# Four stream slots in place of five, one more granule at home, and edits to the first step and the tail

## The chip, the cores and the metric

The kernel runs on one core of a Trainium2 chip. Its time is device time in microseconds (us); three runs of the kernel before gave 1846.27, 1849.24 and 1857.47, and the median, 1849.24, is the figure to compare with. The profile is of one execution. TensorE (PE, with its weight loads as PEld), VectorE (DVE), ScalarE (ACT), GpSimd (POOL) and SyncE (SP) each work through their own instructions in program order, and DMA queues are fed by SP, ACT and POOL. The TensorE clock is granted by a throttle, and the profile shows the granted share as PEclk.

## The reference

`x` is 2048 rows of 1024 numbers. It is normalised (a layer norm without weights), goes through a recurrent attention (A) and through a routed MLP (B), and both are added to it.

```python
def _A_ref(x, mem0, Wq, Wk, Wv, Wo, seg_len):       # 64 segments of 32 rows, 32 heads of 128
    mem = mem0                                       # 8 rows of memory
    for s in range(n_seg):
        xs = x[:, s * seg_len:(s + 1) * seg_len, :].copy()
        h = jnp.concatenate([mem, xs], axis=1)       # 40 rows
        q, k, v = (einsum('btd,dhe->bhte', h, W) for W in (Wq, Wk, Wv))
        scores = jnp.einsum('bhqe,bhke->bhqk', q, k) * scale
        scores = jnp.where(mask[None, None], scores, -1000000000.0)
        o = jnp.einsum('bhqk,bhke->bhqe', _softmax(scores, axis=-1), v)
        o = jnp.einsum('bhte,hed->btd', o, Wo)
        mem = o[:, :M, :].copy()
        outs.append(o[:, M:, :])
    return jnp.concatenate(outs, axis=1)

def _B_ref(x, w_r, w_gate, w_up, w_down):            # the 2 rows with the largest router value
    r = x @ w_r
    idx = jnp.argsort(-r, axis=-1)[:, :C]
    x_sel = jnp.take_along_axis(x, idx_e, axis=1)
    y = (_silu(x_sel @ w_gate) * (x_sel @ w_up)) @ w_down
    ...                                              # times sigmoid(r), added to those rows

x = A_x
xn = _layernorm(x, axis=-1)
return x + _A_ref(xn, A_mem0, A_Wq, A_Wk, A_Wv, A_Wo, A_seg_len) + _B_ref(xn, B_w_r, B_w_gate, B_w_up, B_w_down)
```

Each segment needs the memory that the segment before it left, so the 64 segments run one after the other, and each reads all of Wq, Wk, Wv and Wo.

## The kernel before

**Steps and granules.** One pass of the loop in line 621 is a step: one segment. The weights are cut into 64 granules of 128 x 2048 numbers, 512 KB each. Granules 0 to 47 are Wq, Wk and Wv in six phases of eight (`PHASES`, line 26: Q first half, K first half, Q second half, K second half, V first half, V second half); granules 48 to 63 are Wo. In a phase the state `ST` (32 rows: 24 of x, 8 of memory) is the weight of the matmuls and the granule streams through it, four matmuls side by side (line 745). Line 754 takes a Q or K phase's sum out, line 632 turns it, lines 637 to 642 copy it to `QT` and `KT`. The Wo granules are used in line 798.

**Homes, slots and kept granules.** The on-chip memory can't hold all the weights. 44 granules (`N_RES`) have a home and are loaded once. Three (`KEPT_HERE`: 0, 7, 27) are kept turned in PSUM and brought back each step (line 411). The other 17 (`streamed`, line 77) go through a ring of five slots (`wstream`, `N_SLOT`). `fetch` (line 380) takes the next granule of the list `flow` and issues its load on SP (line 386 in the first step, 388 later, from scratch copies `wsc` that GpSimd makes in the first step). After step 0 a fetch is issued as soon as a streamed granule has been used (`after`, line 575), into that granule's slot, so it is the granule five places on in the list. SP runs in order: a fetch that waits for its slot holds back all that SP has behind it.

**Inside a step.** `hooks` places the attention's parts between granules: scores of the first heads after granule 22 (line 644), their softmax on VectorE and ScalarE (667 to 686), scores of the second heads after granule 38, the weighted sums (`attend`, line 688) after granules 43 and 46 and within the Wo granules. GpSimd loads the next rows of x, the left products (`QKL`) and `VL`.

**Left rows.** Only 24 of a segment's 32 rows go through the loop together with the 8 rows of memory. The last eight of each segment, 512 rows in all, are "left" rows: their products with Wq, Wk and Wv are made in the first step for all segments at once (`left_qk`, line 493, and `left_v`, line 521; in four sets of 128 rows), stored, and loaded per step. Their attention output is stored per step (`store_sums`), loaded back at the end into `OTA`, and multiplied by Wo in `left_rows_out` (line 868): two calls, each of two sets of 128 rows, 64 matmuls a set, the weights read from `OTR` with a stride of 32 numbers.

**First step.** Phase by phase, the eight granules are used for the step itself and then, still in place, for the left products; a slot is released only when both are done. `left_done(p)` (line 548) then fetches one granule for each slot of the phase that has come free, and reloads areas that served as scratch. The row statistics of all x tiles are made on VectorE (line 238); `spread` (line 245) hands them to the segments' rows; `router_tile` (line 261) makes the router value of 128 rows at a time, 16 times, and stands in phase 1, after three heads of left products. `hm` and `hx` are homes that serve as scratch first.

**Tail.** In the last step the homes that are done with take the expert weights (`fetch_moe`, line 429, on SP). `left_sums` (line 852) makes the statistics of the left rows again on VectorE from x loaded on ScalarE's queue (line 850); then come the first call of `left_rows_out`, gate and up products (line 903), the second call, the rest of gate and up, and down (line 930).

Of the kernel before, what the change touches and what calls it, by code (L numbers as in the profile page):

```python
# [8 lines left out]
BF16 = mybir.dt.bfloat16  # L9
# [7 lines left out]

N_RES = 44
N_SLOT = 5
FIRST_KEPT = 0  # L20
NEXT_KEPT = 7
HALF_KEPT = 27
KEPT_HERE = (FIRST_KEPT, NEXT_KEPT, HALF_KEPT)
NEG = -30000.0

# [4 lines left out]
def kernel(  # L30
# [45 lines left out]

    streamed = [1, 4, 11, 15, 21, 23, 29, 34, 37, 41, 45, 47, 50, 54, 56, 58, 63]
    first_streamed = sorted(streamed + list(KEPT_HERE))
# [181 lines left out]

    def router_tile(t):
        XR = home(hx, [P, D], BF16, "XR")
        nc.vector.tensor_scalar(out=XR[:, :], in0=xt(t), scalar1=RI16[:, t, 0:1], scalar2=RI16[:, t, 1:2],
                                op0=ALU.subtract, op1=ALU.mult)
        nc.vector.tensor_tensor_reduce(out=XR[:, :], in0=XR[:, :], in1=WRB, scale=1.0, scalar=0.0,
                                       op0=ALU.mult, op1=ALU.add, accum_out=RF[:, t:t + 1])

# [153 lines left out]
    to_copy = list(streamed)  # L421
    flow += [(s, g) for s in range(NSEG) for g in (streamed if s else first_streamed)]

# [54 lines left out]
    for g in range(KC, 32):  # L478
        if g in first_streamed:
            if len(queued) < N_SLOT:  # L480
                fetch()
        else:
            load_resident(g)
        if g >= 8 and g < 15:
            load_x(g - 7)
    for g in v_homes[8:-1]:
        load_resident(g)
# [5 lines left out]
    def left_qk(mat, half, Gs, between, h0=0, h1=16):  # L493
        if mat == 0 and h0 == 0:
            gathered[half] = area(f"big{half}", [P, NSEG, 256], "GA")
        GA = gathered[half].rearrange("p s (m i q r) -> p s m i q r", m=2, i=4, q=4)
        for h in range(h0, h1):
            PSG = psA.tile([P, 512], F32, tag="acc", name="PSG")
            for kc in range(KC):
                nc.tensor.matmul(PSG[:, :], lhsT=part(Gs[kc], h // 4)[:, P * (h % 4):P * (h % 4 + 1)], rhs=XLT[:, :, kc, :],  # L500
                                 start=(kc == 0), stop=(kc == KC - 1))
            nc.scalar.copy(out=GA[:, :, mat, h % 4, h // 4, :], in_=PSG.rearrange("p (s r) -> p s r", r=XL))  # L502
            if h % 2 == 1 or mat + half == 0:
                next(between, None)
        if h1 < 16:
            return
        for _ in between:
            pass
        if mat == 1:
            G3 = gathered[half]  # L510
            if half == 0:
                qkl[0] = one.tile([P, 2, 2, 4, 4, XL], BF16, tag="bA", name="QKL")
            nc.vector.tensor_copy(out=qkl[0][:, half].rearrange("p m i q r -> p (m i q r)"), in_=G3[:, 0, :])
            if half == 0:
                for k in range(NSEG // 8):
                    store_left(half, k)
# [104 lines left out]
    for s in range(NSEG):  # L621
# [7 lines left out]
        def transposes(mat, half, XB):  # L629
# [8 lines left out]
            else:  # L638
                KT[half] = one.tile([P, 16, NK], BF16, tag="kt", name="KT")
                nc.scalar.copy(out=KT[half].rearrange("p (i q) k -> p i q k", i=4)[:, :, :, 32:NK],  # L640
                               in_=qkl[0][:, half, 1, :, :, :])
                nc.vector.tensor_copy(out=KT[half][:, :, 0:32], in_=pv)  # L642

# [94 lines left out]
        for p, (mat, half) in enumerate(PHASES):  # L738
# [13 lines left out]
            if mat < 2:  # L752
# [4 lines left out]
                if s == 0:  # L757
# [94 lines left out]
    def left_sums():  # L852
# [7 lines left out]
        for t in range(4):  # L860
# [3 lines left out]
            nc.vector.tensor_scalar(out=left_x(t), in0=left_x(t), scalar1=r, scalar2=m, op0=ALU.mult, op1=ALU.add)  # L864

    OTR = OTA.rearrange("p s (r h) -> p (s r) h", h=H)

    def left_rows_out(k):
        WD = [[psK.tile([P, 512], F32, name=f"WD{2 * b + c}", tag=f"kept{2 * b + c}") for c in range(2)] for b in range(2)]
        for b in range(2):  # L870
            for i, (g, Gv) in enumerate(WOS.items()):
                for hs in range(2):
                    for c in range(2):
                        nc.tensor.matmul(WD[b][c][:, :], lhsT=OTR[:, P * (2 * k + b):P * (2 * k + b + 1), 2 * (g - 48) + hs],  # L874
                                         rhs=Gv[:, D * hs + 512 * c:D * hs + 512 * (c + 1)],
# [6 lines left out]

    T0 = room(resident[2], "T0")
    left_sums()
# [87 lines left out]
```

## Time and profile before

| what | value |
|---|---|
| time, median of 3 runs | 1849.24 us (1846.27 to 1857.47) |
| the profiled execution's own time | 1847.92 us |
| its span | 1846.3 us, mean granted clock 0.982 |
| TensorE busy | 1555.7 us (84%) |
| VectorE busy | 880.4 us (48%) |
| ScalarE busy | 774.9 us (42%) |
| GpSimd busy | 320.9 us (17%) |
| DMA moved | 678.50 MB, mean 367 GB/s |

The page's second part cuts the span into 40 slices of 46 us and gives the busy share of each in tenths, so a row of nines is a resource in use all the time. In a row of instructions, the first number is the start, the second the length (of all that are merged, where a count stands at the end), then engine, line, operation, the tiles written and read, shapes and count; in brackets stands the engine's idle time before and what ended it. A row of a waits view has the waiting instruction, what it waited for, the total, the number of times and the longest. A row of a windows view has the stretch, then for PE, PEld, DVE, ACT and POOL the busy time and count, then the granted clock, the DMA share and GB/s.

### The profile page before, as it was taken

The page shows a single profiled execution, that of the slowest core. Times are in us where ns is not written, and L with a number is a line of the kernel's source. Part 1 is how long each engine was busy: PE and PEld are TensorE (multiplying, and loading weights), DVE is VectorE, ACT ScalarE, POOL GpSimd, SP SyncE. Part 2 cuts the span into 40 slices and gives each one's busy share as a digit, 9 for nine tenths or more (in the row PEclk, how much of TensorE's full clock was granted, in tenths as well). Part 3 has the DMA queues.
Part 4 walks back from the last instruction along what each step waited for, and adds up shares of the span by engine and source line. Part 5 has one row for each costly group of instructions (what it writes and reads, how often), then busy time and mean ns, then how long its engine had stood idle before and what let it go on. Part 6 is the DMA issues. An engine that isn't in the chain of part 4 may idle for free. (4 is left out here: it accounts for less than half of the span.)

```text
span 1846.3 us, 70379 instructions
## 1 busy us (share of the span) xinstructions
PE 1555.7 (84%) x30358; PEld 828.2 (45%) x30370; DVE 880.4 (48%) x2711; ACT 774.9 (42%) x2019; POOL 320.9 (17%) x592
## 2 busy tenths in 40 slices
PE   6889978888888888888888888888888888888888
PEld 3334434444444444444444444444444444444465
DVE  6631235555554454555555555444455555555420
ACT  2333134444444444444444444444444444444400
POOL 1020111111111111111111111111111111111200
PEclk9999989999999999999999999999999999999988
DMA  9684899999999999999999999999999999999996
GB/s 361 218 301 135 261 367 391 393 394 394 368 387 376 368 389 383 392 386 372 396 393 396 396 394 394 385 386 389 386 391 394 397 382 393 395 395 395 392 364 251
DMA packets 223288, 678.50 MB, mean 367 GB/s; under 512 B 46848, under 2 KB 54320, under 8 KB 222976
## 3 DMA queue, kind: packets, MB, share of 16 engines
q1 hardware_dynamic: 196768, 623.79, 88.3%
q0 software_dynamic: 24192, 46.54, 7.5%
q8 instruction: 237, 3.88, 0.8%
q10 hardware_dynamic: 2016, 3.67, 0.6%
q14 instruction: 75, 0.61, 0.1%
HBM read 652.90 MB, written 29.89 MB: 370 GB/s over the span
## 5 line engine op out<-in xcount | busy, mean ns | idle before, releaser
L745 PE MATMUL PSm<-wres,ST 128*32 128x512 bf16 x6400 | 500.7, 382 | 0.0
L745 PEld LDWEIGHTS <-ST 128*32 128x32 bf16 x12288 | 313.3, 96 | 349.5 <-issue 107.4
L745 PE MATMUL PSm<-g,ST 128*32 128x512 bf16 x3084 | 307.3, 384 | 46.6 <-DMA g<-wsc 38.2
L411 ACT COPY BK<-KEPT 128x512 bf16<-128x512 bf16 x315 | 189.3, 601 | 175.0 <-PE WO L798 65.1
L798 PEld LDWEIGHTS <-OT 128*32 128x32 bf16 x8192 | 209.2, 97 | 85.6 <-issue 69.3
L754 ACT CAST XB<-PSm 128x512 bf16<-128x512 f32 x256 | 150.2, 587 | 132.7 <-PE PSm L745 131.1
L642 DVE COPY KT<-BT 128x512 bf16<-128x512 bf16 x128 | 51.8, 405 | 290.6 <-PE BT L632 290.6
L798 PE MATMUL WO<-W8B,OT 128*32 128x256 bf16 x4096 | 186.2, 276 | 0.0
L745 PE MATMUL PSm<-W8A,ST 128*32 128x512 bf16 x2048 | 182.7, 380 | 0.0
L587 POOL DMA_DIRECT2D QKL<-ql_d x63 | 46.5, 738 | 755.7 <-ACT OTL L714 740.6
L798 PE MATMUL WO<-g,OT 128*32 128x256 bf16 x2560 | 130.7, 277 | 53.1 <-DMA g<-wsc 48.8
L832 POOL DMA_DIRECT2D out_dram<-XN x256 | 130.7, 526 | 173.9 <-DVE XN L828 173.8
L779 ACT CAST VM<-PSm 128x512 bf16<-128x512 f32 x128 | 80.3, 627 | 114.0 <-PE PSm L745 114.0
L411 DVE COPY BK<-KEPT 128x512 bf16<-128x512 bf16 x189 | 80.2, 425 | 72.3 <-ACT BK L411 36.9
L632 PEld LDWEIGHTS <-XB 128*128 128x128 bf16 x1024 | 57.9, 98 | 106.6 <-ACT XB L754 101.5
L674 DVE TENSOR_REDUCE DN<-BS 128x8 f32<-128x320 f32 x128 | 62.9, 491 | 88.0 <-ACT BS L669 88.0
L632 PE MATMUL BT<-IDENT,XB 128*128 128x128 bf16 x1024 | 101.7, 222 | 3.1
L500 PE MATMUL PSG<-XLT,wres 128*128 128x512 bf16 x352 | 101.3, 390 | 0.8 <-ACT GA L502 0.7
L637 ACT COPY QT<-BT 128x512 bf16<-128x512 bf16 x128 | 74.9, 585 | 53.4 <-PE BT L632 51.4
L659 DVE TENSOR_TENSOR BS<-BS,CT 128x96 f32<-128x96 f32 (+1 forms) x256 | 59.7, 233 | 76.5 <-PE BS L652 72.0
L745 PE MATMUL PSm<-BK,ST 128*32 128x512 bf16 x567 | 76.7, 388 | 22.2 <-DVE ST L369 22.2
L828 DVE CAST XN<-WO 128x256 bf16<-128x256 f32 x64 | 27.2, 424 | 127.5 <-PE WO L798 127.5
(171 smaller groups left out, 2278.9 us busy)
## 6 DMA issues: line engine op xcount, KB each, us to landing
g<-wsc SPq DMA_DIRECT2D x1071, 512.0 KB, 6.3
ql_d<-GA POOLq DMA_DIRECT2D x16, 512.0 KB, 6.3
QKL<-ql_d POOLq DMA_DIRECT2D x63, 128.0 KB, 6.2
MW<-in_B_w_gate_dram SPq DMA_DIRECT2D x16, 448.0 KB, 8.0
MW<-in_B_w_down_dram SPq DMA_DIRECT2D x14, 512.0 KB, 8.3
wres<-in_A_Wk_dram SPq DMA_DIRECT2D x12, 512.0 KB, 10.5
MW<-in_B_w_up_dram SPq DMA_DIRECT2D x12, 448.0 KB, 8.5
XP<-in_A_x_dram SPq DMA_DIRECT2D x8, 512.0 KB, 10.1
```

The lines of the kernel that those rows point to most:

```text
L411: copy(out=back[g][c], in_=KEPT_COLS[g][c])
L500: nc.tensor.matmul(PSG[:, :], lhsT=part(Gs[kc], h // 4)[:, P * (h % 4):P * (h % 4 + 1)], rhs=XLT[:, :, kc, :], start=(kc == 0), stop=(kc = ...
L632: nc.tensor.transpose(out=PTq[:, il, :, :].rearrange("p j r -> p (j r)"), in_=XB[:, il * P:(il + 1) * P], identity=IDENT[:, :])
L637: nc.scalar.copy(out=QT[half][:, :, :], in_=pv)
L642: nc.vector.tensor_copy(out=KT[half][:, :, 0:32], in_=pv)
L659: nc.vector.tensor_tensor(out=S4, in0=S4, in1=m, op=ALU.add)
L674: nc.vector.tensor_reduce(out=DN[:, :], in_=S8, axis=AX.X, op=ALU.add)
L745: nc.tensor.matmul(PSm[32 * jq:32 * jq + 32, :], lhsT=ST[:, kc, :], rhs=part(Gv, jq), start=(kc == 0), stop=(kc == KC - 1), tile_position= ...
L754: nc.scalar.copy(out=XB[:, :], in_=PSm[:, :])
L779: nc.scalar.copy(out=VM[half][:, :], in_=PSm[:, :])
L798: nc.tensor.matmul(PS[32 * g:32 * g + 32, 0:256], lhsT=lhs(h), rhs=Gv[:, D * hs + 256 * g:D * hs + 256 * (g + 1)], start=False, stop=(last ...
L832: nc.gpsimd.dma_start(out=out2[s * SEG:s * SEG + XM, 256 * g:256 * (g + 1)], in_=OB[32 * g:32 * g + XM, :])
```

## The change

**Steady steps.** `N_SLOT` goes from five to four and `N_RES` from 44 to 45; the list of streamed granules has 16 entries instead of 17, at other places.

**First step.** With four slots, granules 0, 1, 5 and 7 fill the ring from the start. Granules 9 and 13, which are also streamed, are loaded in the first step as "guests" into two homes that belong to Wv granules (`v_homes[8]` and `[9]`); at the end of phase 1 they are dropped and the homes get their own granules. Two Wo granules (`o_homes[10:-1]`) are loaded early. The rows' `sd_rows`, `spread` and all 16 router tiles move from the middle of phase 1 to the end of phase 0 (`left_done(0)`), and the router's scratch has two halves. Two copies move from VectorE to ScalarE: that of `qkl` after the left keys, and in the first step the one that fills `KT`.

**Tail.** Before the four matmuls of each granule in `left_rows_out`, VectorE copies the two 128 x 128 weight blocks from the strided `OTR` into one of eight contiguous buffers (`OCS`), and the matmuls read that. `OCS` takes the home that `T0` had; `T0` becomes a small tile of its own.

```diff
-N_RES = 44
-N_SLOT = 5
+N_RES = 45
+N_SLOT = 4
+GUESTS = (9, 13)
...
-    streamed = [1, 4, 11, 15, 21, 23, 29, 34, 37, 41, 45, 47, 50, 54, 56, 58, 63]
+    streamed = [1, 5, 9, 13, 17, 21, 24, 28, 33, 36, 39, 42, 45, 49, 54, 61]
...
-    def router_tile(t):
-        XR = home(hx, [P, D], BF16, "XR")
+    def router_tiles():
+        XR = home(hx, [P, 2, D], BF16, "XR")
+        for t in range(NT):
...
-    flow += [(s, g) for s in range(NSEG) for g in (streamed if s else first_streamed)]
+    flow += [(s, g) for s in range(NSEG) for g in (streamed if s else first_streamed) if s or g not in GUESTS]
...
-        if g in first_streamed:
+        if g in GUESTS:
+            t = res_tiles[g] = room(v_homes[8 + GUESTS.index(g)], "guest")
+            nc.sync.dma_start(out=t, in_=granule_dram(g))
+        elif g in first_streamed:
...
-    for g in v_homes[8:-1]:
+    for g in v_homes[10:-1] + o_homes[10:-1]:
         load_resident(g)
...
-            nc.vector.tensor_copy(out=qkl[0][:, half].rearrange("p m i q r -> p (m i q r)"), in_=G3[:, 0, :])
+            nc.scalar.copy(out=qkl[0][:, half].rearrange("p m i q r -> p (m i q r)"), in_=G3[:, 0, :])
...
         for g in range(8 * p, 8 * (p + 1)):
-            if g in first_streamed:
+            if g in first_streamed and g not in GUESTS:
                 fetch()
-        if p == 1:
+        if p == 0:
+            sd_rows(MV[:, 1:NT, :], VE[:, 1:NT])
+            spread(1, NT)
+            router_tiles()
+        elif p == 1:
+            for i, g in enumerate(GUESTS):
+                res_tiles.pop(g)
+                load_resident(v_homes[8 + i])
...
-                nc.vector.tensor_copy(out=KT[half][:, :, 0:32], in_=pv)
+                (nc.vector.tensor_copy if s else nc.scalar.copy)(out=KT[half][:, :, 0:32], in_=pv)
...
-                        sd_rows(MV[:, 1:NT, :], VE[:, 1:NT])
-                        left_qk(mat, half, Gs, kept, 1, 3)
-                        h1 = 3
-                        spread(1, NT)
-                        for t in range(NT):
-                            router_tile(t)
...
+    OCS = room(resident[2], "OCS").rearrange("p (n h r) -> p n h r", n=8, h=2)
...
             for i, (g, Gv) in enumerate(WOS.items()):
+                OC = OCS[:, (16 * (2 * k + b) + i) % 8]
+                h = 2 * (g - 48)
+                nc.vector.tensor_copy(out=OC, in_=OTR[:, P * (2 * k + b):P * (2 * k + b + 1), h:h + 2].rearrange("p r h -> p h r"))
                 for hs in range(2):
                     for c in range(2):
-                        nc.tensor.matmul(WD[b][c][:, :], lhsT=OTR[:, P * (2 * k + b):P * (2 * k + b + 1), 2 * (g - 48) + hs],
+                        nc.tensor.matmul(WD[b][c][:, :], lhsT=OC[:, hs, :],
...
-    T0 = room(resident[2], "T0")
+    T0 = one.tile([P, 256], BF16, tag="bA", name="T0")
```

More of the change, by code (lines that the diff above doesn't have):

```diff
@@ L259 @@
     hx = v_homes[-1]
-    def router_tile(t):
-        XR = home(hx, [P, D], BF16, "XR")
[L263 to L266, printed above, removed]
+    def router_tiles():
+        XR = home(hx, [P, 2, D], BF16, "XR")
+        for t in range(NT):
+            nc.vector.tensor_scalar(
+                out=XR[:, t % 2, :], in0=xt(t), scalar1=RI16[:, t, 0:1], scalar2=RI16[:, t, 1:2],
+                op0=ALU.subtract, op1=ALU.mult)
+            nc.vector.tensor_tensor_reduce(out=XR[:, t % 2, :], in0=XR[:, t % 2, :], in1=WRB, scale=1.0, scalar=0.0,
+                                           op0=ALU.mult, op1=ALU.add, accum_out=RF[:, t:t + 1])
     def router_out():
```

## The prediction

> **What bounds the kernel now.** I read the whole span first, then one step of the recurrence, then the two ends. "Step" is one of the 64 passes of the segment loop.
>
> ```profile
> span 1846.3 us, 70379 instructions
> DMA  9684899999999999999999999999999999999996
> ...
> DMA packets 166263, 570.07 MB, mean 389 GB/s; under 512 B 25380, under 2 KB 28308, under 8 KB 165982
> ...
> g<-wsc SPq DMA_DIRECT2D x1037, 512.0 KB, 6.3
> ```
>
> The first two lines are the page; the others are the DMA view of the stretch from 266 to 1732 us, steps 2 to 62. There 1037 fetches are 61 steps of 17, so a step takes 1466 / 61 = 24.0 us. The DMA row of the page is full from slice 6 on. One granule of 524 KB at 389 GB/s is 1.35 us of transfer.
>
> ```profile
> PE WO L798 <- DMA g<-wsc: 44.8, 86, 1.8
> PE PSm L745 <- DMA g<-wsc: 37.6, 87, 1.5
> ...
> PE BS L650 <- DVE KT L642: 30.6, 49, 1.0
> PE WO L703 <- ACT OTL L714: 25.1, 45, 0.7
> ...
> DMA to landing us min/median/max: 3.6/6.3/9.2
> ```
>
> These are TensorE's waits in the same stretch (total us, times, longest us), and the last row is from the view of the fetch line L388. TensorE waits 82.4 us for fetched granules, 1.35 us per step: as much as one granule's transfer. So taking one granule of 17 away can save at most about 1.35 us per step by either count, 84 us in the 62 steps between the first and the last. The two waits below these are not the DMA: in 49 and 45 of 61 steps the attention's own chain (scores, softmax, KT copy, sums) holds TensorE, and it stays.
>
> **The change, part by part.**
>
> *The steps between.* Taken away: 1.35 us of transfer per step. Given up: the fifth slot, and with it the lead of a fetch over its use. One step shows what lead there is:
>
> ```profile
> 993.97 0.39 PE L745 MATMUL PSm<-g,ST 128*32 128x512 bf16 x4
> ...
> 995.35 0.40 PE L745 MATMUL PSm<-g,ST 128*32 128x512 bf16 x4 [0.57 <-DMA g<-wsc]
> ...
> 1008.03 0.39 PE L745 MATMUL PSm<-g,ST 128*32 128x512 bf16 x4
> ...
> 1009.30 0.22 PE L703 MATMUL WO<-PT,VL 32*128 32x160 bf16 x1 [0.66 <-ACT OTL L714]
> ...
> 1017.35 0.40 PE L745 MATMUL PSm<-BK,ST 128*32 128x512 bf16 x4 [0.35 <-DVE ST L369]
> ...
> 995.79 1.83 SPq L388 DMA_DIRECT2D g<-wsc  x2
> ```
>
> The rows are granules 1, 4 and 45, the attention after granule 46, the next step's first granule, and SP's issues. Granule 4 came late, at 995.35, and 0.44 us later SP issued the next fetch into its slot: SP hangs on the slots alone. Now, 17 uses share five slots, so a round of one slot is 5 x 24.0 / 17 = 7.06 us, of which 6.3 is issue to landing. After, 16 uses share four slots, four rounds per step. With one request fewer in front, the median landing should fall by 1.35 to 4.95.
>
> The new places count evenly but don't lie evenly in time: thirteen (1 to 45) fall in the 14.06 us from 993.97 to 1008.03, three (49, 54, 61) in the 9.5 us after it. At granule 1 the slots hold 1, 5, 9 and 13. The fetch of 17 leaves 0.44 us later and lands at the least 3.6 us on, at 4.04. Eight more, 21 to 45, follow at 1.35: granule 45 lands at 14.8. TensorE, without the 0.57 wait of today, wants it at 13.5. So 45 is 1.3 us late; the rounds of its slot (1, 17, 33, 45) give the same, 4.04 + 2 x (0.44 + 4.95) = 14.8. A little of this hides under the 0.66 us wait for the sums behind granule 46; landings scatter from 3.6 to 9.2, so I let it hide 0.1. Net per step: -1.35 + 1.2 = -0.15, **-9 us** in all. The ends are wide. If the stretch costs nothing, all of 1.35 is kept: -84. If the landing stays at 6.3 although the queue is shorter, 45 lands at 4.04 + 2 x 6.74 = 17.5, 4.0 late: +164. I take the value nearest to the row of the transfer rate, because the DMA row says the engines, not the issues, set today's landings.
>
> *First step.* Its waits now, and the rows that the edits move:
>
> ```profile
> PE BS L650 <- ACT KT L640: 6.7, 1, 6.7
> PE PSm L745 <- DMA g<-in_A_Wk_dram: 5.5, 1, 5.5
> PE WO L798 <- DMA g<-in_A_Wo_dram: 3.1, 2, 2.8
> ...
> 53.06 0.83 PE L745 MATMUL PSm<-wres,ST 128*32 128x512 bf16 x12
> ...
> 53.44 0.18 DVE L242 TENSOR_SCALAR MISC<-MISC 128x15 bf16<-128x15 bf16 x1
> 68.78 0.87 DVE L255 COPY BS<-BT 96x30 f32<-96x30 f32 x4 [15.16 <-PE BT L250]
> ...
> 98.11 1.23 DVE L265 CUSTOM_DVE_ANT_0 XR<-XR,MISC 128x1024 bf16<-128x1024 bf16 x1
> ...
> 99.40 0.42 DVE L642 COPY KT<-BT 128x512 bf16<-128x512 bf16 x1
> ```
>
> VectorE has the row statistics at 53.44, then idles 15 us until L250, then runs sixteen router tiles up to 99.3, and the first KT copy stands behind them; TensorE waits 6.7 us. Moved to the end of phase 0, the router runs from about 55 to 85, and the KT and QKL copies go to ScalarE besides: -6.3, a copy's length being left over. TensorE is ready at 53.06, before the statistics and the square root behind them; the moved matmuls of L250 make it wait until about 54: +0.9. Granule 15 was fetched only when a slot came free (5.5 us); phase 1 now has all its granules at home or as guests, loaded early: -5.5. The late projection fetches: 49 and 54 go out one phase earlier: -3.1.
>
> What comes late in their place: guests leave nothing to trade in at the end of phase 1, so 28, then 36 and 39, then 45 are fetched at the end of the phase before the one that reads them.
>
> ```profile
> g<-in_A_Wv_dram SPq DMA_DIRECT2D x4, 512.0 KB, 4.3
> ...
> 131.04 0.40 PE L745 MATMUL PSm<-wres,ST 128*32 128x512 bf16 x4
> ...
> 184.31 12.57 SPq L531 DMA_DIRECT2D vl_d<-VG  x8
> 196.97 0.98 SPq L386 DMA_DIRECT2D g<-in_A_Wo_dram  x2
> ...
> 197.11 0.39 PE L745 MATMUL PSm<-g,ST 128*32 128x512 bf16 x4
> ```
>
> Such a fetch takes 4.3 us to land. 28's slot (granule 17's) is released about 1 us before phase 3 starts, so it lands near 133.0 and is wanted at 131.04: +1.9. 36 and 39 go the same way: +1. The worst is 45: on SP it stands behind the eight stores of L531, goes out at 196.97, lands at 201.3 or later and is wanted at 197.11: +4.2, and 5 with other traffic. Together -14.9 + 8.8 = **-6 us**; between -11 (the late fetches cost a third) and +2 (they cost double).
>
> At nothing I cost one copy fewer into scratch memory on GpSimd, which lies beside TensorE's left products, and one home fewer for expert weights in the tail: that piece goes out behind the first call of the left sums and has the second call, 128 matmuls of 0.22, to land in; without that cover it would cost a transfer of 1.2 us.
>
> *Tail.* Sixty-four copies on VectorE now feed the weights of the left sums.
>
> ```profile
> 1755.75 0.62 PE L798 MATMUL WO<-g,OT 128*32 128x256 bf16 x8 [2.19 <-DMA g<-wsc]
> ...
> 1760.19 9.28 PE L874 MATMUL WD<-W8B,OTA 128*128 128x512 bf16 x31 [0.37 <-issue]
> ...
> 1776.22 7.07 PE L874 MATMUL WD<-W8B,OTA 128*128 128x512 bf16 x32
> ...
> 1797.54 1.39 PE L903 MATMUL GU<-RXT,MW 128*128 128x2 bf16 x47 [1.31 <-issue]
> ...
> 1752.34 0.57 ACTq L850 DMA_DIRECT2D XLS<-in_A_x_dram  x1
> ...
> 1770.73 1.29 DVE L238 BATCH_NORM_STATS2 T<-XLS 128x6 f32<-128x512 bf16 x2 [0.43 <-DMA XLS<-in_A_x_dram]
> ...
> 1777.43 0.55 DVE L864 TENSOR_SCALAR XLS<-XLS,T 128x1024 bf16<-128x1024 bf16 x1
> 1777.89 1.28 DVE L880 TENSOR_TENSOR XLS<-XLS,WD 128x512 bf16<-128x512 bf16 x2
> ```
>
> Warm, 32 matmuls take 7.07 us, 0.22 each, with the strided weight loads beside them; contiguous weights can give nothing there, and at the start perhaps 2 us. But the copies stand on VectorE *behind the statistics of the left rows*, whose last input is seen at 1770.73 and whose last instruction ends at 1777.98. The matmuls, which need none of that today, start at 1760.19; they would start after the first copy (0.4, a 128x512 copy's 0.42) at 1778.4: **+18.2**. The waits for the last granules (2.19) don't come back, because the x loads hang on ScalarE's issue at 1752.34. The 1.31 us before L903 goes. In each of the two calls, the second half's first copy also stands behind the two L880 adds: 1.28 + 0.4 + two hand-overs of 0.1 = 1.9, twice 3.7. Sum -1.3 + 18.2 + 3.7 = **+20.6**; from there on TensorE is the end's chain as now. Its ends are +8 (x lands 10 us sooner) and +26 (the two gaps cool the clock, next).
>
> ```profile
> 1760.00:1766.00 6.00, 5.80 (x16) 2.57 (x16) 1.79 (x4) 0.00 (x0) 2.03 (x4) 0.58 1.04 318
> 1766.00:1772.00 6.00, 6.00 (x30) 3.95 (x28) 4.27 (x8) 0.00 (x0) 0.00 (x0) 1.00 1.04 371
> 1798.00:1800.00 2.00, 1.85 (x38) 1.31 (x36) 0.00 (x0) 0.00 (x0) 0.00 (x0) 0.50 1.07 392
> ```
>
> TensorE's granted clock is 0.58 when the sums start and 1.00 six us later, a price paid before and after alike; but it is 0.50 right behind the 1.31 us gap at 1797.54, so a 1.9 us gap may cost 6 us at about half clock, 2.5 lost each. I take 0. The Trainium skill, "TensorE: Matmul & The Clock Gate", section "HAM oscillation — how this bites in real kernels", asks for no idle gap over some 3.4 us; by it the two gaps are free and the sum stays at 20.6. The row at 1798 leans against it, though tiny matmuls went before.
>
> **Sum**, against the profiled execution's 1847.92 us (span 1846.3, 1.3 below the median of 1849.24): 1847.9 - 9 - 6 + 20.6 = 1853.5, say **1854**. One per cent of the median is 18.5 us: about what a measurement can tell from no change.
>
> **Rivals.**
>
> *The cushion isn't needed.* The least landing is 3.6 us; a slot round could then be 0.44 + 3.6 = 4.04, and four slots need only one round in 4 x 1.35 = 5.4 to keep the engines full. Then the whole 84 us come: 1847.9 - 84 - 6 + 20.6 = 1778; with half of it 1820. For it: the full DMA row. Against it: the median landing of 6.3 and nine granules in a row at the transfer's own pace. Chance 0.2. The Trainium skill, "DMA: Bandwidth & Descriptors", section "Anatomy of one DMA — SWDGE (gpsimd) path", gives some 2.0 us fixed plus the bytes over 436 GB/s, an estimate of 3.2 us for a granule; it speaks for this rival, and the trace's least landing of 3.6 is near it, the median not.
>
> *Four slots starve (the other side).* Landings scatter; a late one stops all four slots, and SP can't run ahead. If the landing falls only to 5.3, granule 45 lands at 4.04 + 2 x 5.74 = 15.5, 2.0 late: +0.65 per step, +40, and 1903. It decides from a median landing of about 5.0 on. For it: SP issues only on a released slot. Against it: waits of the attention chain cover a part. Chance 0.25.
>
> *VectorE doesn't hold the sums.* If the x loads land soon after 1752, the tail costs under 5: 1838. For it: the loads are only 1 MB. Against it: today's last is worked on at 1770.73. Chance 0.1. My own case has 0.45.
>
> **How the numbers follow.** My own case runs from 1830 to 1878, by -33 to +15 on the steps; the first rival fills 1778 to 1830, the second 1878 to 1915. Leaving out the lower half of the first and the top of the second gives a range of 1808 to 1898. Faster by over 1% (under 1831): the first rival and a little of the third, 0.23. Slower by over 1% (over 1868): the second and the upper part of my own, 0.36. Within: 0.41.
>
> **What would show it.** In the changed kernel's trace: 16 fetches per step with a median landing near 5.0; TensorE's DMA waits gone from L798 and gathered at granules 39 to 45 of L745; no 6.7 us wait for KT and no 5.5 for granule 15, but 4 to 6 us for 45 in the first step; in the tail TensorE idle some 18 us ahead of L874 with VectorE as releaser, and two gaps of 2 us. I am wrong if the steps run at 22.7 us, if they run above 24.5, or if the left sums start where they do now.

## The result and the profile after

The changed kernel takes 1996.09 us at the median (1992.92 to 2013.52), against 1850.97 us for the kernel before on the same chip: 1.079 times as long, 95% interval 1.0745 to 1.0841. It was forecast at 1854 us, in a range up to 1898. The result lies outside.

I cut each profiled execution at the first weight load of step 1 and of step 63. All kernels of this study stand in this table; the rows below the second are the experiments, beside which the kernel before took 1857 to 1859 us at the median.

| kernel (slots, streamed granules) | first step, us | steps 1 to 62, us per step | step 63 and tail, us | median time, us |
|---|---|---|---|---|
| before (5, 17) | 242.2 | 24.04 | 113.5 | 1850.97 |
| after (4, 16) | 244.2 | 25.91 | 140.8 | 1996.09 |
| five_slots (5, 16) | 226.7 | 24.48 | 139.2 | 1882.32 |
| four_slots_17 (4, 17) | 250.7 | 27.51 | 127.9 | 2081.29 |
| even_places (4, 16) | 242.9 | 25.73 | 139.6 | 1979.01 |
| sums_order (4, 16) | 244.1 | 25.80 | 120.8 | 1970.37 |
| eight_streamed (4, 8) | 244.0 | 22.17 | 135.4 | 1755.41 |
| half_slots (8 halves, 16) | 243.8 | 26.49 | 138.2 | 2025.90 |
| first_step_and_places (5, 17) | 229.4 | 24.07 | 113.0 | 1834.96 |
| half_slots_five (10 halves, 17) | 227.8 | 25.06 | 116.4 | 1898.74 |
| five_slots_even (5, 16) | 230.2 | 23.97 | 136.0 | 1844.73 |
| six_slots_18 (6, 18) | 227.7 | 24.94 | 112.7 | 1892.28 |

Of the 145 us between the first two profiles, 2 lie in the first step, 62 x 1.87 = 116 in the steps between, and 27 in the last step and the tail.

The steps between, after: first the page's span and DMA row, then the DMA view and the waits of TensorE from 270 to 1850 us, and the landing row of the fetch line (now L391). L758 is the main matmul, L805 the projection, L663 the scores, L716 the sums.

```profile
span 1991.3 us, 70371 instructions
...
DMA  9756799999999999999999999999999999999974
...
DMA packets 157432, 537.90 MB, mean 340 GB/s; under 512 B 24400, under 2 KB 27328, under 8 KB 157153
...
g<-wsc SPq DMA_DIRECT2D x976, 512.0 KB, 5.5
...
PE PSm L758 <- DMA g<-wsc: 225.5, 343, 2.9
...
PE WO L805 <- DMA g<-wsc: 6.7, 13, 1.1
...
PE BS L663 <- DVE KT L655: 3.7, 6, 0.7
PE WO L716 <- ACT OTL L727: 0.6, 1, 0.6
...
DMA to landing us min/median/max: 3.5/5.5/7.5
```

TensorE as a whole in steps 2 to 62, before and then after (the windows view; first PE's busy time, near the end the granted clock), and one more wait of the kernel before that is gone:

```profile
266.00:1732.00 1466.00, 1233.64 (x27328) 658.91 (x27328) 743.96 (x2380) 681.18 (x1831) 270.03 (x488) 1.00 1.02 389
270.00:1850.00 1580.00, 1263.42 (x27330) 667.86 (x27330) 748.50 (x2380) 685.62 (x1831) 269.95 (x488) 0.98 0.96 340
...
PE WO L703 <- DMA VL<-vl_d: 15.5, 17, 2.8
```

The page's row of nines looks as before. But the same nines carry 340 GB/s instead of 389, the waits for granules have grown from 82 to 232 us and moved from L798 to the dense stretch, and the two waits of the attention chain (30.6 and 25.1 us before) are nearly gone: they lie under the fetches now. TensorE is also busy 30 us longer with the same work, at a lower granted clock. Per step that makes 2.46 - 0.84 - 0.25 + 0.49 = +1.86: waits for granules, the two attention waits, the wait for `VL`, and the slower TensorE. One step shows where it is late. The rows are TensorE's, granules 17, 24, 33 and 42:

```profile
1024.53 0.40 PE L758 MATMUL PSm<-g,ST 128*32 128x512 bf16 x4 [1.56 <-DMA g<-wsc]
...
1027.14 0.40 PE L758 MATMUL PSm<-g,ST 128*32 128x512 bf16 x4 [0.21 <-DMA g<-wsc]
...
1030.40 0.40 PE L758 MATMUL PSm<-g,ST 128*32 128x512 bf16 x4 [0.62 <-DMA g<-wsc]
...
1035.30 0.40 PE L758 MATMUL PSm<-g,ST 128*32 128x512 bf16 x4 [1.57 <-DMA g<-wsc]
```

The lateness does not gather at 39 to 45 but starts at 17, the first fetch of the step.

TensorE's waits in the first step, after (30 to 246 us):

```profile
PE PSm L758 <- DMA g<-in_A_Wv_dram: 7.5, 2, 5.7
PE PSm L758 <- DMA g<-in_A_Wk_dram: 6.1, 1, 6.1
PE WO L805 <- DMA XLT<-in_A_Wo_dram: 5.5, 1, 5.5
...
PE BT L251 <- ACT MISC L244: 0.8, 1, 0.8
...
PE BS L663 <- ACT KT L655: 0.3, 2, 0.2
```

The 6.7 us for the KT copy and the 5.5 for granule 15 are gone. In their place stand granule 28 (6.1), granules 39 and 45 (1.7 and 5.7) and a projection granule in the `pair` area (5.5).

The tail, in the order of time:

```profile
1893.59 1.28 DVE L239 BATCH_NORM_STATS2 T<-XLS 128x6 f32<-128x512 bf16 x2 [1.13 <-DMA XLS<-in_A_x_dram]
...
1900.30 0.55 DVE L871 TENSOR_SCALAR XLS<-XLS,T 128x1024 bf16<-128x1024 bf16 x1
...
1900.76 2.73 DVE L882 COPY OCS<-OTA 128x256 bf16<-128x256 bf16 x9
...
1901.19 9.48 PE L885 MATMUL WD<-W8B,OCS 128*128 128x512 bf16 x32 [24.40 <-DVE OCS L882]
...
1917.40 1.28 DVE L891 TENSOR_TENSOR XLS<-XLS,WD 128x512 bf16<-128x512 bf16 x2 [6.31 <-PE WD L885]
...
1919.02 7.08 PE L885 MATMUL WD<-W8B,OCS 128*128 128x512 bf16 x32 [1.45 <-DVE OCS L882]
...
1941.58 1.72 PE L914 MATMUL GU<-RXT,MW 128*128 128x2 bf16 x59 [2.58 <-issue]
```

VectorE works through the statistics and the scaling of the left rows up to 1900.85, makes the first copy as that ends, and only then does TensorE start, after 24.4 us of idling. The left sums start 50.7 us after step 63 does; before they started 27.4 us after it.

### The profile page after: what moved, and what is told of

Same layout as the page of the kernel before. It is cut to its first block, busy times and chain, and to the rows that moved or that the text cites. A ratio compares the mean times of both kernels' runs of the same rounds, so it can differ in the third digit from the quotient of the medians.

```text
span 1991.3 us, 70371 instructions
## 1 busy us (share of the span) xinstructions
PE 1587.3 (80%) x30370; PEld 825.1 (41%) x30370; DVE 903.6 (45%) x2771; ACT 781.2 (39%) x2023; POOL 319.9 (16%) x591
## 4 chain that ended last, share of the span: by engine, by line
DMA 52%; PE 42%; DVE 3%; issue 2%; ACT 2%; ACTq 0%; DVEq 0%; SPq 0%
DMA g<-wsc 48%; PE WO L805 12%; PE PSm L758 12%; PE PSG L506 5%; PE WD L885 3%; PE PSV L533 3%; PE BT L348 2%; DVE XN L835 1%; PE BS L716 1%; DMA XLS<-in_A_x_dram 1%; PE WO L358 1%; PE BT L645 1%; ACT OT L725 1%; DMA g<-in_A_Wv_dram 1%; DVE ST L372 1%
## 5 line engine op out<-in xcount | busy, mean ns | idle before, releaser
L758 PEld LDWEIGHTS <-ST 128*32 128x32 bf16 x12288 | 319.1, 96 | 599.1 <-issue 357.7
L758 PE MATMUL PSm<-g,ST 128*32 128x512 bf16 x3332 | 342.2, 393 | 253.9 <-DMA g<-wsc 232.8
L758 PE MATMUL PSm<-wres,ST 128*32 128x512 bf16 x6144 | 525.3, 389 | 0.0
L805 PEld LDWEIGHTS <-OT 128*32 128x32 bf16 x8192 | 206.2, 98 | 42.0 <-issue 27.1
L805 PE MATMUL WO<-W8B,OT 128*32 128x256 bf16 x4096 | 174.8, 278 | 0.0
L758 PE MATMUL PSm<-W8A,ST 128*32 128x512 bf16 x2048 | 174.2, 389 | 0.0
L653 ACT COPY KT<-QKL 128x128 bf16<-128x128 bf16 x128 | 38.1, 298 | 199.3 <-PE BT L645 198.4
L758 PE MATMUL PSm<-BK,ST 128*32 128x512 bf16 x567 | 80.5, 393 | 22.5 <-DVE ST L372 22.5
L506 PE MATMUL PSG<-XLT,wres 128*128 128x512 bf16 x336 | 95.6, 385 | 0.0
L805 PE MATMUL WO<-g,OT 128*32 128x256 bf16 x1536 | 82.3, 277 | 13.8 <-issue 6.7
```

Of the source, the lines that this page charges most:

```text
L758: nc.tensor.matmul(PSm[32 * jq:32 * jq + 32, :], lhsT=ST[:, kc, :], rhs=part(Gv, jq), start=(kc == 0), stop=(kc == KC - 1), tile_position= ...
L805: nc.tensor.matmul(PS[32 * g:32 * g + 32, 0:256], lhsT=lhs(h), rhs=Gv[:, D * hs + 256 * g:D * hs + 256 * (g + 1)], start=False, stop=(last ...
```

## The experiments

**five_slots: the depth of the ring, at the changed kernel's places.**

```diff
-N_SLOT = 4
+N_SLOT = 5
...
+SHARED = 11
...
+        if g == SHARED:
+            res_tiles[g] = res_tiles[g - 1]
...
```

> The changed kernel with its 16 places, but five slots. The memory for the fifth slot is had by giving granule 11 no home: the home of granule 10 is read in its place, so one slice of Wk is computed with a neighbour's weights and the output is another. Theory depth: in the changed kernel a slot's round is 0.44 us (use to issue) + 5.5 (median landing) = 5.94, so four slots bring a granule each 1.49 us, while TensorE can take granules 1 to 45 at one each 14.06 / 12 = 1.17; twelve gaps make 3.8 us of lateness per step. Five slots should be bounded by the transfer again, 1.35 each, 2.2 us of lateness: 1.6 us per step less, 24.3 us per step instead of 25.9, waits for fetched granules below 140 us in 61 steps instead of 232, and about 1897 us (1860 to 1915). Theory places: thirteen of sixteen granules lie in the first 16 us of a step, and no depth of the ring helps: 25.9 us per step, 1985 to 2000 us.

Measured: 1882.32 us, 24.48 us per step; the waits and the DMA view of the steps:

```profile
PE PSm L761 <- DMA g<-wsc: 160.5, 247, 2.3
...
DMA packets 157370, 537.66 MB, mean 360 GB/s; under 512 B 24396, under 2 KB 27324, under 8 KB 157091
...
g<-wsc SPq DMA_DIRECT2D x977, 512.0 KB, 6.1
```

Depth alone gives back 1.43 us per step, of the 1.6 expected; the waits, 160 us, stay above the 140 that were set. The median landing is longer than in the changed kernel (6.1 against 5.5), and yet the steps are shorter: the landing alone is not the measure to look at. The first step falls to 226.7 us too: with a fifth slot the waits for 28, 39 and 45 are gone, and only the `pair` granule's 5.1 us is left. So those three late fetches are the ring's, not the guests'. But 24.48 us with 16 granules is no better than 24.04 with 17: the places cost as well.

**four_slots_17: the depth alone, in the kernel before.**

```diff
-N_SLOT = 5
+N_SLOT = 4
...
-            if s + 1 == NSEG and 48 + w in streamed:
+            if s + 1 == NSEG and 48 + w in streamed and w != 2:
...
```

> The kernel before with its 17 places and four slots; nothing takes the memory that comes free. In the tail the left rows of heads 4 and 5 are multiplied by the weights of granule 48 instead of 50, because four slots can't hold five projection granules to the end; so the left rows' output is another, the time of the products is the same. Theory depth: 17 granules x 1.49 us (0.44 + a landing of 5.5, over four slots) = 25.2 us per step even if no slot ever idles, so 25.2 to 26.5 instead of 24.0 us per step, and 1925 to 2005 us. Theory places: the even spacing of these 17 in time carries it with four slots too: 24.0 to 24.3 us per step and 1851 to 1875 us.

Measured: 2081.29 us, 27.51 us per step, worse than the bound that theory depth gave. The waits of the steps:

```profile
PE PSm L745 <- DMA g<-wsc: 143.5, 202, 2.6
PE WO L798 <- DMA g<-wsc: 117.3, 155, 2.0
```

Even spacing does not carry four slots: 261 us of waits, spread over all matmuls. In the three kernels with four slots the time per granule is one number: 25.91 / 16 = 1.62, 27.51 / 17 = 1.62, 25.73 / 16 = 1.61 us. A slot goes round once in 4 x 1.61 = 6.45 us, in all three: 0.44 from use to issue, 5.5 to 5.6 to land, and the rest until its use. Not all of the 3.5 us per step that this kernel lost is waiting: in steps 2 to 62 TensorE is busy 1321.9 us instead of 1233.6, at a granted clock of 0.94 instead of 1.00. That the ring alone sets the pace is therefore argued from the three equal numbers, and no run holds the clock apart from it.

**even_places: other places, four slots.**

```diff
-GUESTS = (9, 13)
+GUESTS = (9, 12)
...
-    streamed = [1, 5, 9, 13, 17, 21, 24, 28, 33, 36, 39, 42, 45, 49, 54, 61]
+    streamed = [1, 5, 9, 12, 19, 22, 26, 28, 35, 38, 43, 45, 47, 52, 57, 63]
```

> The changed kernel with four slots, but 16 other places: 1, 5, 9, 12, 19, 22, 26, 28, 35, 38, 43, 45, 47, 52, 57, 63, so that eleven instead of thirteen lie up to granule 45 and five after it (guests 9 and 12). Theory depth: with a granule each 1.49 us from four slots 16 take 23.8 us if no slot ever idles, and the stretch 1 to 45 has two granules fewer, 2 x 1.49 us less of supply to wait for, a part of which the later ones give back: 25.0 to 25.4 us per step, about 1953 us (1935 to 1970). Theory places: what the changed kernel lost is the crowd before granule 46, and with it gone the transfer's own 16 x 1.35 = 21.6 and TensorE's work set the step: 22.7 us per step, about 1800 us.

Measured: 1979.01 us, 25.73 us per step. Both theories expected more of it; places are worth at most 0.18 us per step. That is little more than the 0.11 by which sums_order, whose steps are the changed kernel's, differs from it. A ring that brings one granule in 1.61 us at either spacing has little to gain from a better one.

**sums_order: the copies ahead of the statistics.**

```diff
     def left_rows_out(k):
...
+        if k == 0:
+            left_sums()
+        for b in range(2):
             x = left_x(2 * k + b)
...
-    left_sums()
     left_rows_out(0)
```

> The changed kernel with one thing moved in the tail: the first call's copies and products of the left rows are emitted ahead of the left rows' statistics, and the additions behind them; the copies stay. Theory order: TensorE's left sums began 50.7 us after the last step's start because the first copy stood behind the statistics on VectorE; now they begin as in the kernel before, 27 to 29 us after it, and the 1.45 us gap inside the first call goes: 1996 - 24 = 1972 us (1965 to 1978). Rival: something else holds them, the loads of the left outputs or of the last granules, or the copies themselves are too slow for the products: the start moves by less than 10 us and the time stays above 1985.

Measured: 1970.37 us, 26 less. Of the 26.7 us between its profile and the changed kernel's, 20.0 lie in step 63 and the tail; 6.7 lie in the steps before, which the edit doesn't touch, and are scatter. The start of the left sums:

```profile
1876.56 2.74 DVE L882 COPY OCS<-OTA 128x256 bf16<-128x256 bf16 x9 [6.14 <-DMA OTA<-ol_d]
...
1877.39 9.30 PE L885 MATMUL WD<-W8B,OCS 128*128 128x512 bf16 x31 [7.44 <-DVE OCS L882]
...
1893.43 7.07 PE L885 MATMUL WD<-W8B,OCS 128*128 128x512 bf16 x32
```

TensorE's idle time ahead of them falls from 24.40 to 7.44 us, and the 1.45 us gap inside the call is gone. So the order on VectorE cost 17.0 us of start, near the 18.2 that were forecast. The sums still start 33.6 us after step 63 does, not 27 to 29: the first copy waits 6.1 us for the stored left outputs (`OTA`). GpSimd issues their loads 17.9 us into step 63 in the changed kernel and 14.0 us into it before; these are the rows, before and then after:

```profile
1746.79 5.96 POOL L595 DMA_DIRECT2D OTA<-ol_d  x8 [11.26 <-PE PSm L745]
...
1868.39 5.96 POOL L608 DMA_DIRECT2D OTA<-ol_d  x8 [15.14 <-PE BT L719]
```

With the right order the tail is still 7 us longer than before (120.8 against 113.5). Six of these are the later start. From the start of the sums on it takes 87.2 us against 86.1, and 32 matmuls take 7.07 us as before, so the contiguous weights gain nothing.

**eight_streamed: what a fetch costs by itself.**

```diff
+    SHARE = (5, 13, 21, 28, 36, 42, 49, 61)
...
-        if g in streamed:
+        if g in streamed and (s == 0 or g not in SHARE):
             fetch()
...
+            for i, g in enumerate(SHARE):
+                res_tiles[g] = res_tiles[v_homes[i] if g < 48 else o_homes[i]]
```

> The changed kernel with four slots, but from the second step on only granules 1, 9, 17, 24, 33, 39, 45 and 54 are fetched; the places of 5, 13, 21, 28, 36, 42, 49 and 61 read granules that have a home, so from there on those products use other weights and the output is another. It measures what a fetch costs that has the engines nearly to itself. Three kernels with four slots had one and the same time per slot round: 25.91 x 4 / 16 = 6.48, 27.51 x 4 / 17 = 6.47 and 25.73 x 4 / 16 = 6.43 us. Theory own latency: a fetch alone takes 4.5 to 5.0 us at the median, so that most of that round is there without any queue. Theory queue (the prediction's): a fetch alone takes 3.6 to 3.9, and the rest of the 5.5 is made by the requests in front. Both: TensorE no longer waits for fetches, 21.9 to 22.3 us per step, 1996 - 62 x 3.8 = 1760 us (1745 to 1775).

Measured: 1755.41 us, 22.17 us per step, with no wait for fetches. The fetch line's landing row from 300 to 1600 us:

```profile
DMA to landing us min/median/max: 3.1/4.1/5.5
```

The median of 4.1 lies between the two theories. The completion records by granule decide it: granules 24 and 33 are requested 0.2 and 1.1 us after the fetch ahead of them has landed (medians), and both land in 3.3 us; the others, requested 1.4 to 2.5 us before the fetch ahead has landed, take 4.1 to 4.7. So a lone fetch is as short as the prediction thought; theory own latency falls, and the rest of the 5.5 comes with the company. The Trainium skill, "DMA: Bandwidth & Descriptors", section "Anatomy of one DMA — SWDGE (gpsimd) path", gives some 2.0 us fixed plus the bytes over 436 GB/s for a DMA issued by GpSimd, an estimate of 3.2 us for a granule; these fetches go out by SP, and the lone ones agree with it, while those in company don't. The step of 22.17 us is what TensorE and the attention chain need when every granule is there: 2 us of the kernel before's 24.04 hang on the stream.

**half_slots and half_slots_five: the same bytes in smaller pieces.**

```diff
-    wstream = ctx.enter_context(tc.tile_pool(name="wstream", bufs=N_SLOT))
+    wstream = ctx.enter_context(tc.tile_pool(name="wstream", bufs=2 * N_SLOT))
...
-            nc.sync.dma_start(out=t[:, :], in_=wsc[g][:, :])
+            for c in range(2):
+                nc.sync.dma_start(out=t[c], in_=wsc[g][:, D * c:D * (c + 1)])
```

> The changed kernel with the same memory for the ring cut into eight slots of half a granule, each fetch as two requests of 256 KB, nothing else changed. Theory slot round: time per granule is the round, 6.48 us, over four; a half lands about half a transfer earlier (5.5 - 0.67 = 4.8) and gives its half slot back earlier, so the round falls to about 5.8, 1.45 us per granule, 16 x 1.45 = 23.2 if no slot idles: 24.0 us per step and about 1878 us (1850 to 1920). Rival: what a fetch takes is the same whatever its size, so half as much comes in the same time from each of twice as many slots: 25.9 us per step and 1985 to 2000; or the 2 KB rows cost more than 4 KB rows: above 2000.

> The kernel of the run before this one with ten half slots instead of five slots. Theory slot round: the round of 24.04 x 5 / 17 = 7.07 us falls by half a transfer, 0.67, to 6.4, 1.28 us per granule, under the transfer's own 1.35; so the transfer is the only bound, 17 x 1.35 = 22.95, with other traffic 23.3 us per step: some 12 to 45 us faster than that run. Rival: with five slots the ring is deep enough and the DMA engines are what is full; no difference beyond 10 us, or slower by the smaller rows.

Measured: 2025.90 us (26.49 per step) and 1898.74 us (25.06 per step), against 25.91 and 24.07 for whole slots. These rows are the matmuls on streamed granules from 300 to 1700 us, in the changed kernel and in half_slots (busy time, mean ns, then idle time before them), and the DMA view of half_slots in the same stretch:

```profile
L758 PE MATMUL PSm<-g,ST 128*32 128x512 bf16 x2816 | 289.2, 393 | 206.6 <-DMA g<-wsc 200.4
...
L772 PE MATMUL PSm<-g,ST 128*32 128x512 bf16 x2748 | 446.1, 386 | 152.2 <-DMA g<-wsc 140.8
...
DMA packets 258618, 466.97 MB, mean 334 GB/s; under 512 B 34723, under 2 KB 37255, under 8 KB 258365
...
g<-wsc SPq DMA_DIRECT2D x1694, 256.0 KB, 5.3
```

The times are those of the rivals, but not for the rivals' reason. The waits for granules fall, from 3.81 to 2.72 us per step with four slots' memory and from 1.63 to 1.45 with five. What grows is TensorE's own busy time, from 20.7 to 22.3 and from 20.5 to 22.0 us per step. With whole granules the four matmuls of a granule start within 0.02 us of each other and run side by side; with halves the second two start 0.43 us after the first two on average (0.28 with ten half slots). So these two runs don't settle whether smaller requests help the ring. They do show that 2 KB rows carry less per busy time of the DMA engines: 334 GB/s at a share of 0.98 against 341 at 0.96, and 373 at 1.04 against 389 at 1.01.

**first_step_and_places: the part of the change that is worth having.**

```diff
-    streamed = [1, 4, 11, 15, 21, 23, 29, 34, 37, 41, 45, 47, 50, 54, 56, 58, 63]
+    streamed = [1, 8, 12, 17, 20, 25, 29, 33, 38, 40, 42, 46, 48, 52, 56, 59, 63]
...
-            nc.vector.tensor_copy(out=qkl[0][:, half].rearrange("p m i q r -> p (m i q r)"), in_=G3[:, 0, :])
+            nc.scalar.copy(out=qkl[0][:, half].rearrange("p m i q r -> p (m i q r)"), in_=G3[:, 0, :])
...
-        if p == 1:
+        if p == 0:
+            sd_rows(MV[:, 1:NT, :], VE[:, 1:NT])
+            spread(1, NT)
+            router_tiles()
+        elif p == 1:
...
-                nc.vector.tensor_copy(out=KT[half][:, :, 0:32], in_=pv)
+                (nc.vector.tensor_copy if s else nc.scalar.copy)(out=KT[half][:, :, 0:32], in_=pv)
```

> The kernel before, five slots and 17 granules, with the early router and the KT and QKL copies on ScalarE, and with the places 1, 8, 12, 17, 20, 25, 29, 33, 38, 40, 42, 46, 48, 52, 56, 59, 63; tail as before. First step: the 6.7 us wait for the KT copy goes (-6.3 + 0.9), and granules 8 and 12 fill the ring from the start, so the 5.5 us wait for granule 15 goes too, and some late fetches come: about -8, 234 instead of 242 us. Steps: theory places: the 1.35 us of waits for granules per step shrink with spacing nearer to TensorE's own times, 24.04 to 23.5 us: 1851 - 8 - 33 = 1810 us (1800 to 1835). Rival: the waits are the transfer's own, 389 GB/s, and no place helps: 24.0 us per step and 1843 us (1836 to 1850).

Measured: 1834.96 us, 0.9875 times the kernel before (95% interval 0.9846 to 0.9904): faster than both. It comes from the first step, 229.4 instead of 242.2 us; its waits for the KT copy and for a Wk granule are gone. The steps stay at 24.07 us, so the rival of that expectation holds for the steps: at five slots and 17 granules these places gain nothing over the old ones.

**five_slots_even: both, five slots and the other places.**

```diff
-N_SLOT = 4
+N_SLOT = 5
...
-    streamed = [1, 5, 9, 13, 17, 21, 24, 28, 33, 36, 39, 42, 45, 49, 54, 61]
+    streamed = [1, 5, 9, 12, 19, 22, 26, 28, 35, 38, 43, 45, 47, 52, 57, 63]
...
```

> The 16 more even places (1, 5, 9, 12, 19, 22, 26, 28, 35, 38, 43, 45, 47, 52, 57, 63) with five slots; as in the earlier run with five slots, granule 11 has no home and granule 10's is read in its place, so that slice of Wk is a neighbour's. With four slots these places gave 25.73 instead of 25.91 us per step. Theory interaction: with four slots the ring itself sets 1.61 us per granule wherever the granules lie, so places can't help; with five it can bring one in 1.41 (24.04 / 17), 16 x 1.41 = 22.6 against TensorE's own 22.2 (the run with eight granules), and then the places decide: 23.0 instead of 24.48 us per step, 1882 - 62 x 1.45 = 1792 us (1780 to 1815). Rival: places are worth as little with five slots as with four: 24.3 us per step and about 1870 us.

Measured: 1844.73 us, 23.97 us per step. The places are worth 0.5 us per step here and 0.18 with four slots; the direction is that of theory interaction, the size is a third of it. Part of the 0.5 is the clock: the mean granted from 300 to 1700 us is 0.97 in five_slots and 0.99 here. Even with five slots and 16 granules the steps are where the kernel before has them with 17. The completion records say where the rest is: granules 38 to 47 land 7.3 to 7.6 us after their requests, and TensorE waits for 38 in 54 and for 45 in 43 of 61 steps.

**six_slots_18: the other way.**

```diff
-N_RES = 44
-N_SLOT = 5
+N_RES = 43
+N_SLOT = 6
...
-    streamed = [1, 4, 11, 15, 21, 23, 29, 34, 37, 41, 45, 47, 50, 54, 56, 58, 63]
+    streamed = [1, 8, 12, 16, 19, 22, 25, 29, 33, 37, 40, 42, 46, 48, 52, 56, 59, 63]
...
```

> The kernel with the new first step, with one granule less at home: six slots, 43 homes and 18 streamed granules (1, 8, 12, 16, 19, 22, 25, 29, 33, 37, 40, 42, 46, 48, 52, 56, 59, 63); it computes what the reference does. Theory engines: with five slots the DMA engines are in use all the time (share 1.02, 389 to 392 GB/s), so a sixth slot gives a few per cent of rate at most (340 with four, 389 with five, say 402): 1.414 x 389 / 402 = 1.37 us per granule, 18 x 1.37 = 24.6 us per step instead of 24.07, 1835 + 33 = 1868 us (1855 to 1890). Rival: the slot round of 7.07 us is what binds with five too, and stays: 7.07 / 6 = 1.18 us per granule, the step falls towards TensorE's own time, 23.0 us, and 1835 - 66 = 1769 us.

Measured: 1892.28 us, 24.94 us per step. The rival (a fixed slot round) is out: the round is 6 x 24.94 / 18 = 8.3 us, not 7.07. Theory engines had the direction, and its range ended 2 us too low. Time per granule falls only from 1.42 to 1.39, and the eighteenth granule costs more than that: 24.94 against 24.07 us per step in the kernel it was made from. Of the kernels tried with four, five and six slots in this memory, those with five are the fastest.

**The rate by depth.** These rows are the windows view from 1000 to 1700 us of eight_streamed, four_slots_17, the kernel before and six_slots_18; the last three columns are the clock, the DMA share and GB/s.

```profile
1000.00:1700.00 700.00, 595.83 (x13257) 329.75 (x13252) 376.69 (x1193) 322.94 (x868) 134.11 (x241) 0.98 0.67 214
```

```profile
1000.00:1700.00 700.00, 550.59 (x11504) 284.40 (x11504) 315.64 (x1009) 288.01 (x772) 112.96 (x204) 0.95 0.96 342
```

```profile
1000.00:1700.00 700.00, 592.98 (x13178) 315.82 (x13174) 359.59 (x1149) 327.33 (x878) 129.99 (x235) 1.00 1.02 392
```

```profile
1000.00:1700.00 700.00, 582.12 (x12573) 304.64 (x12574) 343.69 (x1096) 316.16 (x842) 125.44 (x228) 1.00 1.02 396
```

A share of 0.96 reads as full, yet a full share is worth 214 / 0.67 = 319 GB/s, 342 / 0.96 = 356, 392 / 1.02 = 384 and 396 / 1.02 = 388 in the four. Between the second and the third only the number of slots differs.

## Why the prediction was wrong, step by step

**The steps between: the cost was named, and priced at almost nothing.** The prediction named the lost lead as the cost, saw that the waits would move to the dense stretch, and bounded the cost at +164 us; 116 came. Its own value of -9 rests on granule 45 being 1.3 us late, and that failed in three places of one sum.

- *"With one request fewer in front, the median landing should fall by 1.35 to 4.95"*: it fell to 5.5. The 1.35 us was the transfer at 389 GB/s, and that rate was itself a product of five slots. With four it is 340, which is 1.54 us per granule.
- *"At granule 1 the slots hold 1, 5, 9 and 13"*: two of them are still on their way. By the completion records granule 1 is used 0.2 us after the start of the step, while 9 lands at 1.4 and 13 at 3.3 (medians). So the fetch of 17, sent at 0.7, has two others in front of it.
- *"lands at the least 3.6 us on"*: the least was used for the usual. The fetch of 17 lands in 4.9 us at the median, and 3.3 is had only by a fetch that is alone.

With the measured sizes the prediction's formula gives 0.44 + 4.9 + 2 x (0.44 + 5.5) = 17.2 us for granule 45, wanted at 13.5: 3.7 late. The trace has 232.2 / 61 = 3.8 us of waits for granules per step, where the prediction had 1.2. So the form of the sum held for the waits, and its sizes did not. Two terms stood at nothing. The attention's waits were to stay and went (-0.84 per step), and so did the wait for `VL` (-0.25). And TensorE ran slower: with the longer waits the granted clock fell, +0.49 per step or 30 us in the steps. One place shows the clock:

```profile
313.58 0.40 PE L758 MATMUL PSm<-g,ST 128*32 128x512 bf16 x4 [1.82 <-DMA g<-wsc]
...
315.50:318.90 3.40, 3.40 (x60) 2.23 (x58) 0.75 (x3) 1.21 (x5) 0.00 (x0) 0.50 0.86 282
```

The rival "four slots starve" was the one that happened. Its landing of 5.3 was close, but its price of +40 took over the 3.6 and the full slots.

**One granule less is worth 1.35 us per step**: not even with the depth kept. five_slots and five_slots_even have 16 granules and 24.48 and 23.97 us per step against 24.04, so at these places it is worth 0.07 at most. The -1.35 stands in the prediction's own sum as well as in its end of -84. "The cushion isn't needed" fell with four_slots_17, where the fifth slot alone was taken and the step grew by 3.5 us.

**First step: forecast -6, measured +2.** The gains for the KT copy and granule 15 came as forecast (6.7 to 0.3 and 5.5 to 0), so did the price of the moved `spread` (0.8 for 0.9) and that of granule 45 (5.7 for 5), and 36 with 39 (1.7 for 1). Two terms were mis-sized. Granule 28 was priced at 1.9 and cost 6.1: by its completion record it took 8.7 us to land, not the 4.3 of the sum. The -3.1 for the projection granules came, but the second granule of the `pair` area, loaded at the end of phase 5 behind the fetches, is now 59 instead of 61, wanted earlier, and is waited for 5.5 us instead of 1.2. With five slots all these edits are worth -15.5 (five_slots), and without the guests -12.8 (first_step_and_places).

**Tail: forecast +20.6, measured +27.3.** The hold behind the statistics was right in cause and size (18.2; 17.0 by sums_order). The gaps were 1.45 us each, not 1.9. Two parts were missing: the later start of the last step's loads, which the prediction took to be as early as before (6.2), and the wait ahead of the gate and up products (L903, now L914), which was to go and grew from 1.31 to 2.58. Together 17.0 + 6.2 + 2.9 + 1.3 = 27.4.

Both 1.45 us gaps were followed by a granted clock of 1.00, so they cooled nothing. The first two rows are the stretches behind them, the third is the kernel before around its 1.31 us gap, all from the windows view:

```profile
1919.00:1925.00 6.00, 5.98 (x28) 2.75 (x29) 4.09 (x13) 0.00 (x0) 0.00 (x0) 1.00 0.18 46
...
1960.50:1966.50 6.00, 6.00 (x28) 2.74 (x29) 4.11 (x13) 0.00 (x0) 0.00 (x0) 1.00 0.59 216
...
1790.00:1798.00 8.00, 6.68 (x252) 6.59 (x251) 1.28 (x2) 0.00 (x0) 0.00 (x0) 0.65 1.16 323
```

The row at 1798, which the prediction set against this, was misread. A mean of 0.65 over the 8 us before it means half clock for 5.6 of them, so the clock had fallen about 5 us before the matmul at 1797.54, during the 128x2 matmuls of L903. The rule of the Trainium skill, "TensorE: Matmul & The Clock Gate", section "HAM oscillation — how this bites in real kernels", that no idle gap over some 3.4 us should be left, agrees with these two gaps. It doesn't cover the steps of the same trace, where the clock fell to half behind the 1.82 us wait shown above, and the longest wait of all is 2.9 us.

## What to carry to other kernels

Price a ring of buffers by the time of one slot's round and the bytes in flight, never by the transfer rate that the deeper ring happens to show: here that rate fell with the depth, and a DMA share near 1 hid the fall. Count the clock too: here the waits cost more than their sum, because matmuls behind them ran slower. Taking a slot to save a transfer is a trade of rate for bytes; try it from the row of GB/s per share, and against the step with the stream almost gone. And when copies are put on an in-order engine, look up what stands ahead of them there.

## What the runs showed of the hardware

The DMA engines move less when fewer bytes are queued: by the number of slots alone the rate falls from 392 to 342 GB/s. In the packet records from 300 to 1700 us a 4 KB packet takes 159, 160 and 161 ns at the median with four slots (four_slots_17), five (before) and six; but one packet in a hundred takes over 761 ns, 373 and 261. Counted by packets under way against 16 engines, an engine has no packet in 5.9% of the time with four slots and 0.9% with five. That fits engines which run out of queued packets and lose time when the next request starts. In eight_streamed, where requests come nearly alone, 29% of the 4 KB packets that begin 0.8 to 1.6 us after a request take over 300 ns, and 5% of the others. No run isolates such a start, so the cause of the long packets is argued, not shown.

TensorE's granted clock fell to half for stretches of mostly 3.4 us without any long idle gap: 18 times in steps 2 to 62 of the changed kernel, 45 times in four_slots_17 and 3 times before. In the 3.41 us ahead of each, TensorE had idled 1.2 to 2.7 us.
